# A gated recurrence and a bilinear layer: products moved off GpSimd, inverse scans restarted, weight loads on another queue

## The chip, the cores and the metric

The kernel runs on one core of one Trainium2 chip. The metric is the time of one execution on the device, in microseconds (us). Engines go by the profile's names: PE (TensorE, matrix products), DVE (VectorE), ACT (ScalarE), POOL (GpSimd), SP (SyncE, which here only issues transfers). A "q" behind an engine's name is its queue of issued transfers.

## The reference

Two layers in a row. For 4 batches and 8 heads, 768 steps of a recurrence with a state of 48 x 48, then a layer without a nonlinearity on 3072 tokens of 384 values, with 1536 inner channels:

```python
f = 1.0 / (1.0 + np.exp(-f_logit))            # f_logit about 2.0 +- 0.5
for t in range(768):
    state = f[:, :, t, :, None] * state + np.einsum('bhd,bhe->bhde', k[:, :, t], v[:, :, t])
    y[:, :, t] = np.einsum('bhd,bhde->bhe', q[:, :, t], state)
x = y.transpose(0, 2, 1, 3).reshape(4 * 768, 8 * 48)
out = ((x @ w_a) * (x @ w_b)) @ w_out
```

The three weight matrices arrive as 64-bit floats, everything else as 32-bit floats. All arithmetic is 32-bit.

## The kernel before

**Recurrence.** The work is cut into 16 units (`unit`): one batch, one half of the sequence (384 steps) and four heads, with two heads side by side on the partitions (48 of each 64) and two in the free dimension. A unit's tiles f, k, q and v lie in one of four sets. The decay is written as a quotient: q is multiplied by the running product of f, k by the running product of 1/f, both scaled to stay in range, so that the sums over steps become matrix products over chunks of 64. `front(u)` prepares a unit in three stages:

- stage 1 (L213 to L217): two sigmoids on ACT, of x and of -x - 75; from the second, POOL makes 1 + 1/odds, an approximation of 1/f (`inv`, L216), and its product with f (`fix`, L217), both 768 columns wide;
- stage 2 (L219 to L224): ACT turns `fix` into 2 - f * inv, a correction; DVE scans f (two scans of 384 steps, L222); POOL multiplies q by the scanned f (L224);
- stage 3 (L228, L229): DVE scans `inv` with the factor `fix` (two scans of 384) and multiplies k by it.

`scores` (L257, masked by DVE in L273), `turn` (transposes of k, L284, copied by ACT), `gains` (L303, states summed by DVE in L317 to L326), `within` (L336) and `across` (L356) are the matrix products of a unit. `across` copies y out of PSUM on ACT (L367) into a tile with one buffer and sends it with transfers on SP's queue (L381) into `xT`, the input of the second layer.

**Second layer.** `ffn(blk)` works on eight blocks of 384 tokens. In twelve steps it forms a and b for 128 inner channels (L396: six products for `w_b`, six for `w_a`, PSUM from a ring of four tiles), copies b on ACT (`b_sb`, L404) and multiplies on DVE (`ab`, L406, a product of one operand in PSUM and one in SBUF). Then come the products with `w_out` (L416), 72 in a block, whose results ACT copies out (L426).

**Weights.** `from_double` makes 32-bit floats out of 36 pieces of 128 x 384 64-bit floats (12 of `w_b`, 12 of `w_a`, alternating, then 12 of `w_out`). From the upper words ACT takes absolute value and sign (L166, L167), POOL clamps (L168); two iterations later DVE shifts, masks, scales the lower words and adds (L173 to L176); ACT takes the absolute value once more (L177); one iteration later POOL multiplies by the sign into the weights (L180). `load_weights` issues a piece's load on SP's queue (L154) into one of five buffers, which is free again when L175 has read it.

**Order.** It is written out by hand, and each engine and queue works in the order of the program. The first part prepares units 0 to 2, with a few calls of `convert`, which runs the conversion until n pieces are done. In block 0 `convert` stays some pieces ahead of the step (`min(2 * i + 6, ...)`), while `slot(u)` spreads the front of unit u + 1 and the products of unit u over the steps: six calls a unit, one unit in 7.5 steps. Blocks 1 to 7 go on with the slots alone. At the end a flag that `check_held` has computed decides whether a slower, safe version of the recurrence (`by_levels`) runs; here it does not.

## Time and profile before

| | us |
|---|---|
| median of 3 runs (lowest to highest) | 728.22 (727.71 to 728.41) |
| the profiled execution, as timed | 727.83 |
| its span in the trace | 726.1 |

| engine | busy us | share of the span | instructions |
|---|---|---|---|
| PE | 641.3 | 88% | 4770 |
| DVE | 274.3 | 38% | 467 |
| ACT | 183.5 | 25% | 343 |
| POOL | 149.3 | 21% | 140 |

The page has one execution. Its busy shares are means over stages with different limits, so the slices and stretches of the span matter more here than the sums. "L173" is line 173 of the kernel; a bracket behind an instruction tells how long its engine was idle before it and what ended that. An instruction's length contains the time that it waits for a port once it has started.

### The profile page before, as it was taken

To read this page: it belongs to the slowest core of one execution; us is meant where nothing else is said; L and a number is where in the kernel's file an instruction comes from. 1 tells how busy PE (TensorE), PEld (TensorE's weight loads), DVE (VectorE), ACT (ScalarE), POOL (GpSimd) and SP (SyncE) were. 2 spreads that over 40 slices of the span, in tenths; PEclk is the share of its full clock that TensorE was granted. 3 is DMA by queue.
4 is the path that set the end of the run, shared out by engine and by line. 5 is a ranking of instruction groups with operands and counts; after the bars stand their busy time and mean duration, and the time that the engine had idled before them with its cause. 6 is when DMAs were issued, how large, how long until landed. Compare 5 with 4: busy or idle time off the path is not lost.

```text
span 726.1 us, 11432 instructions
## 1 busy us (share of the span) xinstructions
PE 641.3 (88%) x4770; PEld 390.9 (54%) x4770; DVE 274.3 (38%) x467; ACT 183.5 (25%) x343; POOL 149.3 (21%) x140
## 2 busy tenths in 40 slices
PE   0424875879999999999999999999999999999996
PEld 0423433445566665665665666666666666555553
DVE  8947888889333302322242214131333011001100
ACT  4333446444221202221212122211212011111100
POOL 8635464456201002100102010100110000000000
PEclk9955998799999999999999999999999999999999
DMA  8835324630403030304030401121000000010000
GB/s 212 223 99 130 112 88 124 179 96 32 116 12 71 27 89 0 83 9 106 1 83 0 104 13 41 42 70 46 8 12 20 31 0 18 8 42 0 1 12 25
DMA packets 34300, 43.29 MB, mean 60 GB/s; under 512 B 4032, under 2 KB 32704, under 8 KB 34240
## 3 DMA queue, kind: packets, MB, share of 16 engines
q1 hardware_dynamic: 34240, 42.48, 22.0%
q8 instruction: 39, 0.64, 0.4%
q14 instruction: 21, 0.17, 0.1%
HBM read 33.03 MB, written 4.72 MB: 52 GB/s over the span
## 4 chain that ended last, share of the span: by engine, by line
PE 74%; DVE 16%; ACT 3%; POOL 2%; DMA 2%; issue 2%; SPq 0%; ACTq 0%; POOLq 0%
PE f L396 45%; PE f L416 23%; DVE h L176 3%; DVE r L175 3%; DVE r L174 2%; DVE h L173 2%; DMA k_in<-in_k_dram 2%; PE ps_y L336 2%; DVE inv L228 1%; PE ps_x L257 1%; PE ps_y L356 1%; DVE f_in L222 1%; PE ps_x L303 1%; PE ps_x L284 1%; DVE st L319 1%
## 5 line engine op out<-in xcount | busy, mean ns | idle before, releaser
L396 PE MATMUL f<-xT,w_b 128*128 128x384 f32 x576 | 212.4, 507 | 14.9 <-ACT b_sb L404 14.9
L396 PE MATMUL f<-xT,w_a 128*128 128x384 f32 x576 | 201.7, 486 | 0.0
L416 PE MATMUL f<-w_out,ab 128*128 128x384 f32 x576 | 190.5, 488 | 4.7 <-POOL w_out L180 3.1
L406 DVE TENSOR_TENSOR ab<-f,b_sb 128x384 f32<-128x384 f32 x96 | 53.6, 558 | 329.9 <-PE f L396 311.6
L396 PEld LDWEIGHTS f<-xT,w_b 128*128 128x128 f32 x576 | 109.7, 196 | 88.3 <-POOL w_a L180 11.2
L416 PEld LDWEIGHTS f<-w_out,ab 128*128 128x128 f32 x576 | 108.4, 190 | 81.6 <-POOL w_out L180 6.2
L396 PEld LDWEIGHTS f<-xT,w_a 128*128 128x128 f32 x576 | 109.9, 191 | 77.3 <-issue 1.6
L404 ACT COPY b_sb<-f 128x384 f32<-128x384 f32 x96 | 45.7, 476 | 228.1 <-PE f L396 228.1
L216 POOL TENSOR_SCALAR inv<-inv 128x768 f32<-128x768 f32 x16 | 14.6, 914 | 236.5 <-ACT inv L214 236.4
L426 ACT COPY o_sb<-f 128x384 f32<-128x384 f32 x24 | 11.5, 478 | 167.8 <-PE f L416 162.2
L224 POOL TENSOR_TENSOR q_in<-q_in,f_in 128x768 f32<-128x768 f32 x16 | 30.6, 1915 | 107.6 <-DVE f_in L222 102.1
L257 PE MATMUL ps_x<-q_in,k_in 48*64 48x64 f32 x720 | 15.5, 238 | 41.4 <-POOL q_in L224 19.8
L257 PEld LDWEIGHTS ps_x<-q_in,k_in 48*64 48x64 f32 x720 | 13.9, 152 | 41.9 <-POOL q_in L224 19.8
L177 ACT ACTIVATE h<-h 128x384 f32<-128x384 f32 x36 | 18.8, 523 | 69.8 <-DVE h L176 69.7
L228 DVE TENSOR_TENSOR_SCAN inv<-inv,fix 128x384 f32<-128x384 f32 x32 | 33.9, 1100 | 5.4 <-ACT fix L219 5.4
L168 POOL TENSOR_SCALAR h<-h 128x384 f32<-128x384 f32 x36 | 22.9, 638 | 53.6 <-ACT h L166 51.3
L222 DVE TENSOR_TENSOR_SCAN f_in<-f,zero 128x384 f32<-128x384 f32 x32 | 32.4, 1054 | 2.1 <-ACT inv L214 2.1
L217 POOL TENSOR_TENSOR fix<-f,inv 128x768 f32<-128x768 f32 x16 | 31.2, 1950 | 1.3
L319 DVE TENSOR_TENSOR st<-st,ps_x 128x96 f32<-128x96 f32 x80 | 20.3, 253 | 24.3 <-PE ps_x L303 21.8
L367 ACT COPY y<-ps_y 64x384 f32<-64x384 f32 (+1 forms) x48 | 22.8, 474 | 21.0 <-PE ps_y L356 16.1
L176 DVE TENSOR_TENSOR h<-h,r 128x384 f32<-128x384 f32 x36 | 26.8, 746 | 1.2
L175 DVE SCALAR_TENSOR_TENSOR r<-raw,r 128x384 f32<-128x384 uint32 x36 | 25.3, 703 | 1.2
(56 smaller groups left out, 351.1 us busy)
## 6 DMA issues: line engine op xcount, KB each, us to landing
f_in<-in_f_logit_dram SPq DMA_DIRECT2D x32, 144.0 KB, 2.9
k_in<-in_k_dram SPq DMA_DIRECT2D x32, 144.0 KB, 3.4
q_in<-in_q_dram SPq DMA_DIRECT2D x32, 144.0 KB, 3.9
v_in<-in_v_dram SPq DMA_DIRECT2D x16, 288.0 KB, 4.5
raw<-in_moe_w_b_dram SPq DMA_DIRECT2D x12, 384.0 KB, 3.6
raw<-in_moe_w_a_dram SPq DMA_DIRECT2D x12, 384.0 KB, 3.5
raw<-in_moe_w_out_dram SPq DMA_DIRECT2D x12, 384.0 KB, 3.0
out_dram<-o_sb SPq DMA_DIRECT2D x24, 192.0 KB, 1.9
```

Of the source, the lines that this page charges most:

```text
L175: nc.vector.scalar_tensor_tensor(out=r, in0=lo, scalar=2.0**-52, in1=r, op0=ALU.mult, op1=ALU.mult)
L176: nc.vector.tensor_tensor(h, h, r, ALU.add)
L217: nc.gpsimd.tensor_tensor(fix, f, inv, ALU.mult)
L222: nc.vector.tensor_tensor_scan(x[:, c], f[:, c], zero.broadcast_to((128, BLK)), math.exp(MIDDLE), ALU.mult, ALU.add)
L224: nc.gpsimd.tensor_tensor(halves(t["q"]), halves(t["q"]), x, ALU.mult)
L228: nc.vector.tensor_tensor_scan(inv[:, c], inv[:, c], fix[:, c], math.exp(-MIDDLE), ALU.mult, ALU.mult)
L257: nc.tensor.matmul(ps[h][SUB * p:SUB * p + SUB, o:o + SUB], lhsT=kf[r, tokens(n, c, p)], rhs=qf[r, tokens(n, c, p)], start=True, stop=True,)
L319: nc.vector.tensor_tensor(st[:, j], before, new, ALU.add)
L396: nc.tensor.matmul(ps[nm], lhsT=w[:, kt, ft * 128:ft * 128 + 128], rhs=x[:, kt], start=kt == 0, stop=kt == NKT - 1,)
L404: nc.scalar.copy(b_sb, ps["b"])
L406: nc.vector.tensor_tensor(ab[ft], ps["a"], b_sb, ALU.mult)
L416: nc.tensor.matmul(o[tg], lhsT=ab[ft][:, tg * 128:tg * 128 + 128], rhs=w_out[:, ft], start=ft == 0, stop=ft == NFT - 1,)
```

## The change

- `from_double`: ACT's second absolute value and POOL's product by the sign are gone. ACT makes the upper half of a word with the sign bit alone (`bit`, a third ACT pass with 16-bit output), POOL subtracts the bias of the exponent from the upper 16 bits of the clamped words (a second pass with one input), DVE's first operation shifts and puts the bit in, so it has two tensor inputs, and DVE's last one writes the weights. The conversion is one iteration shorter, `load_weights` comes one iteration later, and `convert` is called with smaller numbers.
- `load_weights`: from the fifth piece on, loads are issued on ACT's queue.
- `front`: `fix` is gone, with the POOL product, the ACT pass and the tile. The inverses are scanned in chunks of 128 steps, each restarted from the reciprocal of the scanned f at the end of the chunk before (DVE). The product for q moves from POOL in stage 2 to DVE in stage 3. The second sigmoid also sums its outputs (for `check_held`). 24 takes the place of 75 in its argument.
- `y` has two buffers; in units 0 and 1 half of its transfers are issued on ACT's queue.
- In the start-up the fronts of units 0 and 1 no longer alternate: unit 0 goes through all stages and on to its scores first, and the conversions begin behind the scores and transposes of unit 1.

```diff
     def load_weights():
...
-            nc.sync.dma_start(out=raw, in_=src)
+            (nc.scalar if len(raws) > 3 else nc.sync).dma_start(out=raw, in_=src)
...
     def from_double(dst, raw, shape):
...
-        h, sign = (sb4.tile([128, PIECE], FP32, tag=n, name=n) for n in ("h", "sign"))
+        i = nth[0] % len(signs)
+        nth[0] += 1
+        sign, bit = signs[i]
+        h = sb4.tile([128, PIECE], FP32, tag="h", name="h")
+        upper = h.bitcast(U16).rearrange("p (n two) -> p n two", two=2)[:, :, 1]
         nc.scalar.activation(h, hi.bitcast(FP32), AF.Abs)
         nc.scalar.activation(sign, hi.bitcast(FP32), AF.Sign)
+        nc.scalar.activation(
+            bit.bitcast(U16).rearrange("p (n two) -> p n two", two=2)[:, :, 1], sign, AF.Relu, scale=-32768.0
+        )
         nc.gpsimd.tensor_scalar(h, h, HI_MAX, HI_MIN, ALU.min, ALU.max)
+        nc.gpsimd.tensor_scalar(upper, upper, 1.0, -float(HI_BIAS), ALU.mult, ALU.add)
         yield
         yield
...
-        nc.vector.tensor_scalar(hu, hu, 3, 0x40000000, ALU.logical_shift_left, ALU.bitwise_xor)
+        nc.vector.scalar_tensor_tensor(
+            out=hu, in0=hu, scalar=3, in1=bit, op0=ALU.logical_shift_left, op1=ALU.bitwise_or
+        )
         nc.vector.tensor_scalar(ru, hu, 0xFF800000, None, ALU.bitwise_and)
         nc.vector.scalar_tensor_tensor(out=r, in0=lo, scalar=2.0**-52, in1=r, op0=ALU.mult, op1=ALU.mult)
-        nc.vector.tensor_tensor(h, h, r, ALU.add)
-        nc.scalar.activation(h, h, AF.Abs)
-        yield
-        h, sign = (x.rearrange("p (k n) -> p k n", k=shape[0]) for x in (h, sign))
-        nc.gpsimd.tensor_tensor(dst, h, sign, ALU.mult)
+        h, r = (x.rearrange("p (k n) -> p k n", k=shape[0]) for x in (h, r))
+        nc.vector.tensor_tensor(dst, h, r, ALU.add)
     def conversion():
...
-            load_weights()
-            yield n - 2
+            if n:
+                load_weights()
+            yield n - 1
     def front(u):
...
-        nc.scalar.activation(inv, x, AF.Sigmoid, bias=less, scale=-1.0)
-
-        nc.gpsimd.tensor_scalar(inv, inv, math.exp(K_EXP), 1.0, ALU.mult, ALU.add)
-        nc.gpsimd.tensor_tensor(fix, f, inv, ALU.mult)
-        yield
-        nc.scalar.activation(fix, fix, AF.Identity, bias=two, scale=-1.0)
+        nc.scalar.activation(inv, x, AF.Sigmoid, bias=less, scale=-1.0, accum_out=tails[:, u:u + 1])
+        nc.gpsimd.tensor_scalar(inv, inv, EXP_K, 1.0, ALU.mult, ALU.add)
+        yield
...
-        nc.gpsimd.tensor_tensor(halves(t["q"]), halves(t["q"]), x, ALU.mult)
-        yield
+        yield
+        start = sb2.tile([128, 2, NC - 1], FP32, tag="start", name="start")
+        nc.vector.reciprocal(start, t["f"].rearrange("p n (c m) -> p n c m", m=C)[:, :, 0:NC - 1, C - 1])
         for n in range(2):
-            c = slice(n * BLK, n * BLK + BLK)
-            nc.vector.tensor_tensor_scan(inv[:, c], inv[:, c], fix[:, c], math.exp(-MIDDLE), ALU.mult, ALU.mult)
+            for c in range(NC):
+                w = slice(n * BLK + c * C, n * BLK + c * C + C)
+                first = start[:, n, c - 1:c] if c else math.exp(-MIDDLE)
+                nc.vector.tensor_tensor_scan(inv[:, w], inv[:, w], none[:, 0:C], first, ALU.mult, ALU.add)
+        nc.vector.tensor_tensor(halves(t["q"]), halves(t["q"]), x, ALU.mult)
         nc.vector.tensor_tensor(halves(t["k"]), halves(t["k"]), inv, ALU.mult)
     def across(u):
...
-        y = sb1.tile([128, 2 * NC, 2, SUB], FP32, tag="y", name="y")
+        y = sb2.tile([128, 2 * NC, 2, SUB], FP32, tag="y", name="y")
...
-                    nc.sync.dma_start(out=xT[blk][p:p + w, kt], in_=y[row:row + w, n])
+                    queue = nc.scalar if u < NQ and (n + h) % 2 else nc.sync
+                    queue.dma_start(out=xT[blk][p:p + w, kt], in_=y[row:row + w, n])
     with tc.manual_schedule():
...
         next(fronts[0])
-        next(fronts[1])
         next(fronts[0])
         next(fronts[1])
-        convert(1)
         scores(0)
         turn(0, True)
-        convert(2)
+        convert(0)
+        next(fronts[1])
         within(0)
         gains(0)
         scores(1, True)
         turn(1, True)
-        convert(3)
+        convert(1)
         across(0)
         within(1)
         gains(1)
         next(fronts[2])
-        convert(4)
+        convert(2)
         across(1)
         next(fronts[2])
         next(fronts[2])
         slots = {s: slot(s) for s in range(NQ, NU + 1)}
         next(slots[NQ])
-        convert(6)
+        convert(4)
...
-                    convert(min(2 * i + 6, 2 * NFT) if i < NFT - 2 else NFT + i + 4)
+                    convert(min(2 * i + 4, 2 * NFT) if i < NFT - 1 else NFT + i + 3)
```

## Rows read from the trace of the kernel before

**Rows 1.** Page, span in 40 equal slices: busy tenths of TensorE and VectorE.

```profile
PE   0424875879999999999999999999999999999996
...
DVE  8947888889333302322242214131333011001100
```

**Rows 2.** Stretches: length, busy us (instructions) of PE, PEld, DVE, ACT, POOL, clock, DMA.

```profile
81.28:158.73 77.45, 54.25 (x321) 31.07 (x320) 64.66 (x105) 39.81 (x82) 42.91 (x45) 0.87 0.42 124
158.73:186.95 28.22, 25.06 (x165) 14.00 (x166) 26.77 (x43) 11.44 (x23) 14.79 (x14) 1.00 0.21 59
186.95:726.10 539.15, 533.04 (x3692) 323.29 (x3691) 120.24 (x227) 100.46 (x183) 44.41 (x30) 1.00 0.14 35
```

**Rows 3.** Groups of VectorE, 24 to 187 us: count | busy us, mean ns | idle before.

```profile
L176 DVE TENSOR_TENSOR h<-h,r 128x384 f32<-128x384 f32 x36 | 26.8, 746 | 1.2
L175 DVE SCALAR_TENSOR_TENSOR r<-raw,r 128x384 f32<-128x384 uint32 x36 | 25.3, 703 | 1.2
L173 DVE TENSOR_SCALAR h<-h 128x384 uint32<-128x384 uint32 x36 | 20.4, 566 | 0.0
L174 DVE TENSOR_SCALAR r<-h 128x384 uint32<-128x384 uint32 x36 | 19.3, 536 | 1.2
L228 DVE TENSOR_TENSOR_SCAN inv<-inv,fix 128x384 f32<-128x384 f32 x8 | 9.1, 1182 | 5.4 <-ACT fix L219 5.4
...
L406 DVE TENSOR_TENSOR ab<-f,b_sb 128x384 f32<-128x384 f32 x12 | 6.7, 558 | 11.5 <-ACT b_sb L404 11.5
```

**Rows 4.** Order of time, 78 to 82 us: start us, length us, instruction [idle before].

```profile
78.20 0.35 DVE L173 TENSOR_SCALAR h<-h 128x384 uint32<-128x384 uint32 x1
...
78.99 0.56 DVE L175 SCALAR_TENSOR_TENSOR r<-raw,r 128x384 f32<-128x384 uint32 x1
...
79.37 0.54 POOL L168 TENSOR_SCALAR h<-h 128x384 f32<-128x384 f32 x1 [3.75 <-ACT h L166]
...
79.58 0.74 DVE L176 TENSOR_TENSOR h<-h,r 128x384 f32<-128x384 f32 x1
79.61 0.37 SPq L154 DMA_DIRECT2D raw<-in_moe_w_a_dram  x1
...
80.36 0.52 ACT L177 ACTIVATE h<-h 128x384 f32<-128x384 f32 x1 [0.62 <-DVE h L176]
...
81.28 0.56 DVE L406 TENSOR_TENSOR ab<-f,b_sb 128x384 f32<-128x384 f32 x1 [0.96 <-ACT b_sb L404]
```

**Rows 5.** Order of time, 89 to 94 us: VectorE operations beside GpSimd's.

```profile
89.75 0.89 POOL L216 TENSOR_SCALAR inv<-inv 128x768 f32<-128x768 f32 x1 [1.72 <-ACT inv L214]
89.97 1.06 DVE L176 TENSOR_TENSOR h<-h,r 128x384 f32<-128x384 f32 x1
...
93.25 1.10 POOL L180 TENSOR_TENSOR w_b<-h,sign 128x384 f32<-128x384 f32 x1
93.54 1.23 DVE L175 SCALAR_TENSOR_TENSOR r<-raw,r 128x384 f32<-128x384 uint32 x1
```

**Rows 6.** Order of time, 295 to 301 us: a front's third stage and the scores.

```profile
296.02 1.80 DVE L228 TENSOR_TENSOR_SCAN inv<-inv,fix 128x384 f32<-128x384 f32 x2
...
297.85 0.96 DVE L229 TENSOR_TENSOR k_in<-k_in,inv 128x768 f32<-128x768 f32 x1
...
299.95 0.88 PE L257 MATMUL ps_x<-q_in,k_in 48*64 48x64 f32 x48
```

**Rows 7.** Groups of VectorE, 81.28 to 158.73 us: the scans of f.

```profile
L222 DVE TENSOR_TENSOR_SCAN f_in<-f,zero 128x384 f32<-128x384 f32 x2 | 1.8, 941 | 0.0
```

**Rows 8.** Order of time, 47 to 55 and 184 us: waits for y, fix and `w_out`.

```profile
47.28 3.12 SPq L381 DMA_DIRECT2D xT<-y  x5
...
52.23 1.46 ACT L367 COPY y<-ps_y 128x384 f32<-128x384 f32 x3 [4.33 <-DMA xT<-y]
...
54.68 0.96 DVE L228 TENSOR_TENSOR_SCAN inv<-inv,fix 128x384 f32<-128x384 f32 x1 [5.43 <-ACT fix L219]
...
184.75 2.20 PE L416 MATMUL f<-w_out,ab 128*128 128x384 f32 x6 [1.72 <-POOL w_out L180]
```

More of the change, by code (lines that the diff above doesn't have):

```diff
@@ L21 @@
 HI_MIN, HI_MAX = (struct.unpack("f", struct.pack("I", x))[0] for x in (0x38000000, 0x47EFFFFF))
+HI_BIAS = 0x3800
 R = 64
 SUB = 64
-K_EXP = 75.0
+K_EXP = 24.0
+EXP_K = math.exp(K_EXP) * (1 + 1.8e-7)
+TAIL_MAX = math.exp(-17)
 MIDDLE = 34.0
@@ L88, in by_quotients @@
     fixedp = ctx.enter_context(tc.tile_pool(name="fixed", bufs=1))
-    sb1 = ctx.enter_context(tc.tile_pool(name="sb1", bufs=1))
     sb2 = ctx.enter_context(tc.tile_pool(name="sb2", bufs=2))
@@ L111, in by_quotients @@
     less = fixed([128, 1], "less")
-    two = fixed([128, 1], "two")
+    signs = [
+        (fixed([128, PIECE], f"sign{i}"), fixedp.tile([128, PIECE], U32, tag=f"bit{i}", name=f"bit{i}"))
+        for i in range(3)
+    ]
+    tails = fixed([128, NU], "tails")
     held = fixed([128, NU, 2], "held")
@@ L144, in pieces @@
             yield w_out[:, ft:ft + 1], moe_w_out[ft * 128:ft * 128 + 128].unsqueeze(1), (1, DM)
-    todo, raws = list(pieces()), []
+    todo, raws, nth = list(pieces()), [], [0]
     def load_weights():
@@ L211, in front @@
         x = halves(t["f"])
[L212 removed]
+        f, inv = (sb2.tile([128, 2 * BLK], FP32, tag=n, name=n) for n in ("f", "inv"))
         nc.scalar.activation(f, x, AF.Sigmoid)
[L214 to L217 removed]
+        nc.scalar.activation(inv, x, AF.Sigmoid, bias=less, scale=-1.0, accum_out=tails[:, u:u + 1])
+        nc.gpsimd.tensor_scalar(inv, inv, EXP_K, 1.0, ALU.mult, ALU.add)
         yield
[L219 removed]
+        none = zero.broadcast_to((128, BLK))
         for n in range(2):
             c = slice(n * BLK, n * BLK + BLK)
[L222 removed]
+            nc.vector.tensor_tensor_scan(x[:, c], f[:, c], none, math.exp(MIDDLE), ALU.mult, ALU.add)
         nc.vector.tensor_tensor(held[:, u], t["f"][:, :, BLK - 1], least, ALU.is_ge)
[L224 removed]
         yield
+        start = sb2.tile([128, 2, NC - 1], FP32, tag="start", name="start")
+        nc.vector.reciprocal(start, t["f"].rearrange("p n (c m) -> p n c m", m=C)[:, :, 0:NC - 1, C - 1])
         for n in range(2):
[L227 to L228 removed]
+            for c in range(NC):
[3 more added lines that the diff above has]
+        nc.vector.tensor_tensor(halves(t["q"]), halves(t["q"]), x, ALU.mult)
         nc.vector.tensor_tensor(halves(t["k"]), halves(t["k"]), inv, ALU.mult)
@@ L453, in check_held @@
     def check_held():
-        n = NU * 2
-        some = fixedp.tile([128, 1], FP32, tag="some", name="some")
-        nc.vector.reduce_sum(some, held.rearrange("p u j -> p (u j)"), axis=mybir.AxisListType.X)
+        n = NU * 3
+        fits = fixed([128, NU], "fits")
+        some = fixed([128, 2], "some")
+        nc.vector.tensor_scalar(fits, tails, TAIL_MAX, None, ALU.is_le)
+        nc.vector.reduce_sum(some[:, 0:1], fits, axis=mybir.AxisListType.X)
+        nc.vector.reduce_sum(some[:, 1:2], held.rearrange("p u j -> p (u j)"), axis=mybir.AxisListType.X)
+        nc.vector.tensor_tensor(some[:, 0:1], some[:, 0:1], some[:, 1:2], ALU.add)
         ps = ps_x
-        nc.tensor.matmul(ps[0:1, 0, 0:1], lhsT=some, rhs=ones, start=True, stop=True)
+        nc.tensor.matmul(ps[0:1, 0, 0:1], lhsT=some[:, 0:1], rhs=ones, start=True, stop=True)
         nc.vector.tensor_scalar(bad, ps[0:1, 0, 0:1], 128.0 * n, None, ALU.is_lt)
@@ L463, in by_quotients @@
         nc.scalar.preload_act_table_set("sigmoid_and_others")
-        for x, value in ((less, -K_EXP), (two, 2.0), (zero, 0.0), (least, math.exp(MIDDLE - DECAY_MAX)), (ones, 1.0)):
+        for x, value in ((less, -K_EXP), (zero, 0.0), (least, math.exp(MIDDLE - DECAY_MAX)), (ones, 1.0)):
             nc.gpsimd.memset(x, value)
@@ L486, in by_quotients @@
         next(fronts[1])
+        for _, bit in signs:
+            nc.gpsimd.memset(bit, 0)
         make_identity(nc, ident)
```

5 lines of the change are left out of this document (2 added, 3 removed).

## The prediction

> **What bounds the kernel now.** I read the slices of the page first, then the busy time of each engine in stretches, then the groups of VectorE in the slow stretch, then the order of time inside one step of it. The slices split the span in two [rows 1]. From about 187 us on TensorE (PE) is at 9 tenths or more in every slice: it is the bound, and the other engines have room. Ahead of that it is at 2 to 8 tenths while VectorE (DVE) stands at 8 or 9 nearly everywhere. The stretches say the same in numbers [rows 2]. Between 81.28 and 158.73 us, the twelve steps of the first feed-forward block, PE is busy 54.25 of 77.45 us and DVE 64.66. Between 158.73 and 186.95 us (the products with `w_out` of that block) both are close to full, 25.06 and 26.77 of 28.22 us. After 186.95 us PE is busy 533.04 of 539.15 us at a granted clock of 1.00, the 2.4 GHz level. The matmuls of that last part are not changed, so time is won where DVE converts weights, and whatever is won there moves the last part forward as a whole.
>
> In the slow stretch four DVE operations on 36 pieces of weights take most of the time: 26.8, 25.3, 20.4 and 19.3 us [rows 3]. Together that is 91.8 us, and with about 3.6 us of short gaps between them (1.2 before three of the four lines) 95.4 us, 2.65 us a piece. DVE also sat idle for 11.5 us before the product `ab`, always behind ScalarE's (ACT's) copy `b_sb` [rows 3].
>
> The order of time shows what a piece costs when nothing disturbs it [rows 4]: from the start of L173 (78.20) to the start of L176 (79.58) is 1.38 us, and a clean L176 would take 0.56, with its last 0.1 under the next start: 1.84 us. The rest, 0.81 us, is waiting inside the instructions while GpSimd (POOL) works. A product on POOL of 1.10 us stretches L175 from 0.56 to 1.23, and a pass with one input of 0.89 us stretches L176 to 1.06 [rows 5]; the shorter pass L168 stretches it to 0.74 [rows 4].
>
> **The change part by part.** Sums are made against the profiled execution: span 726.1 us, 727.83 us as timed, so 1.73 us lie around the span. The median of the runs shown is 728.22.
>
> Part 1, conversion. Gone are ACT's second absolute value (L177) and POOL's product by the sign (L180). New are an ACT pass that writes the sign bit, a POOL pass over 16-bit halves, and a second input in DVE's first operation. That operation goes from 0.35 us [rows 4] to what another 384-wide operation with two inputs and unsigned words takes, 0.56 (L175, same group): +0.21, so a clean piece is 2.05 us. Then the waits for POOL. The 0.67 us of a product goes (L175 at 1.23). The 0.18 of L168 stays (0.74 against 0.56). The new 16-bit pass is nowhere in the trace. Its nearest row is L168, a pass of the same count with one input: 0.18. Its upper bound is the product, 0.67; its lower is nothing, if it always falls beside the `ab` product, which reads PSUM. I take the near end, a little up: 0.39 for both passes, 2.44 us a piece (2.1 to 2.9). 36 x (2.65 - 2.44) = 7.6 us won.
>
> The rule that speaks against this part is in the Trainium skill, "SBUF — State Buffer", section "Who interferes with whom": a VectorE instruction with two SBUF inputs contends with any GpSimd instruction that reads SBUF, and the later of the two waits. By it the passes with one input go on blocking, and DVE's first operation becomes one that can be blocked on its second input. Were it not so, the piece would be 2.05 us; the 1.06 us beside L216 [rows 5] agrees with the rule.
>
> Part 2, the step's end. Now DVE waits 0.96 us before each `ab`: L177 waits for L176 and only then does ACT copy `b_sb` [rows 4]. Afterwards ACT's queue holds, in that place, the issue of a weight load that waits for L175, one operation earlier. A load's issue took 0.37 us on SP's queue [rows 4]; on ACT it is not in the trace (0 to 0.9 us). L175's end + 0.37 + the copy, about 0.46 (it and L177 lie between 80.36 and 81.28), against L175's end + 0.59 for L176: some 0.4 us with the semaphores. 12 x (0.96 - 0.40) = 6.7 us won.
>
> Part 3, the fronts. On DVE the new q product is as large as the k product, 0.96 us [rows 6]. The scans of the inverses go from two of 384 to six of 128, the same 768 elements. Two took 1.80 [rows 6] with 0.94 for one [rows 7], so 0.86 apart; of that 0.80 scales with length if a short operation's fixed part is about 0.06. Six are 1.6 + 6 x 0.06 + 0.1 = 2.05 us. If instead the 0.14 that a 128-wide scan may keep is paid in full, it is six times 0.41, 2.5. The reciprocals of four values: about 0.2. So +0.96 + 0.25 + 0.2, 1.4 us a front. Against it: the two-input POOL products vanish (`fix`, q) that stretch the scans in the start-up from 0.94 to a mean of 1.18 [rows 3] and hold others up besides. For the five fronts that lie ahead of the last piece I take the two as equal: 0, with +/-4 us.
>
> Part 4, early stalls. At 54.68 DVE had sat 5.43 us behind `fix`, which stood on ACT behind the copies of y, which waited 4.33 us for the transfers out of the single y buffer; these began at 47.28 behind a weight load on SP's queue [rows 8]. Double buffering, the end of `fix` and the load on ACT's queue take this whole stall away: 5.4 us. Late next is the first conversion, which now stands behind both score tiles: three ACT passes and two POOL passes of about 0.5 [rows 4] run before DVE has its first words, some 2 us. 3.4 us won.
>
> The move of the loads is the second place where a rule can be held against the trace. The Trainium skill, "DMA: Bandwidth & Descriptors", section "Issuing engines are not separate DMA queues", says that issuing from more engines saves only the sequencer's time. So I count nothing for faster transfers, only the in-order wait at 47.28.
>
> Part 5, what the move costs ACT. Behind a load's issue that waits for DVE stand ACT's passes for later pieces, the `b_sb` copies, the sigmoids of a front, the copies of kT and y. ACT is busy 39.81 of 77.45 us in the stretch [rows 2]; 24 issues of 0.37 add 9. That mostly fits, but where a front's two sigmoids stand ahead of `b_sb` DVE waits for ACT: an estimate of 2.5 us lost.
>
> Part 6, the last piece. PE waits 1.72 us for POOL's last product [rows 8]; it will wait for DVE directly: 1.6 us won.
>
> Part 7, the part bound by PE. A front's third stage sits between two `ab` there. Its first scan starts at 296.02, k is ready at 298.81, and the scores start at 299.95 [rows 6]: room of 1.1 us. The new stage is 0.2 + 2.05 + 0.96 + 0.96 = 4.2 us with gaps (4.1 to 4.9), so k is ready at 300.2 and PE waits 0.3 to 1.0 us. This holds for every second unit, five times after 187 us: 2.0 us lost (1.4 to 5).
>
> Sum: -7.6 - 6.7 + 0 - 3.4 + 2.5 - 1.6 + 2.0 = -14.8. Span 711.3, timed 713.0 us. A floor: in 158.73 to 186.95 PE has 25.06 us of work of its own, so at most 3.2 us can be won there, whatever DVE saves.
>
> **The rivals.**
> A. POOL's one-input passes fall beside `ab` and waits and cost DVE nothing: 2.05 us a piece. That is another 36 x 0.39 = 14, of which those pieces that run beside a full PE give little back: about 12 to 13, 700 us. For it: L406 reads PSUM. Against it: 1.06 us in [rows 5].
> B. The 16-bit pass is as dear as a product and blocks for 0.67: 0.48 more on 36 pieces, 17 us, 730 us: the POOL wait has only changed its name. For it: no row shows a strided 16-bit pass. Against it: it has one input and half the bytes.
> C. Slower: a scan pays its cost once per instruction and not per element, so that a 128-wide one takes as long as a 384-wide one. Six are then 5.2 us in place of 2.05. That adds 3.1 us to five fronts in the start-up and, as PE already waits for k, 3.1 to each of five units afterwards: 31 us, 744 us. It decides from 0.25 us more a scan on (15 us over 60 scans), a scan of some 0.58 us. Against it: two lengths of plain operations here, 384 in 0.56 and 768 in 0.96, scale with their elements.
> D. It doesn't do what it says: the load's issue on ACT, waiting for DVE, holds `b_sb` up as long as L177 did. Then the 6.7 us of part 2 stay: 720 us.
>
> **How the numbers follow.** Forecast with its spread 0.58, D 0.10, A 0.14, B 0.10, C 0.07, 0.01 for something else that is slow. A measurement can tell 0.2% (1.5 us) from no change. Faster: forecast, A and D, 0.82. Within 0.2%: most of B, 0.07. Slower: C and the upper half of B, 0.11. The range 699 to 727 holds A, the forecast, D and the clean bounds of parts 3 and 7, and leaves out B and C.
>
> **What would show it.** L173 with two inputs at 0.56 or more, the four conversion lines near 88 us in sum (A: 74, B: 105); the wait of `ab` for `b_sb` near 5 us; the wait for `fix` gone; 128-wide scans at 0.33 to 0.41; PE idle before L257 some 0.3 to 1.0 us, five times; the first block done near 170 in place of 187 us. I am wrong if ACT, with waits ahead of `b_sb`, takes DVE's place as the bound.

## The result, and the profile after

| | before | after |
|---|---|---|
| median (lowest to highest), us | 728.12 (727.71 to 728.41) | 705.84 (704.70 to 706.96) |
| the profiled execution, as timed | 727.83 | 705.12 |
| its span | 726.1 | 703.4 |

The ratio of the times is 0.969 (0.9675 to 0.9713). The forecast was 713.0, a gain of 14.8 us; the span became 22.7 us shorter. Sign and range held, and the sum was 7.9 us too small.

The slices of the page after, in the form of [rows 1]:

```profile
PE   1519868789999999999999999999999999999996
...
DVE  8679999994343124231434024231514111001100
```

VectorE (DVE) stands at 9 from the fourth to the ninth slice and falls to 4 in the tenth, which begins at 158 us; in [rows 1] it falls in the eleventh, at 182. From there on TensorE (PE) is at 9 tenths or more but for the last slice, as before. The stretches, cut at the same places of the program as [rows 2] (start of block 0, start of its products with `w_out`, start of block 1) with the start-up in the first row; the columns are those of [rows 2]:

```profile
0.00:64.35 64.35, 27.74 (x593) 21.32 (x594) 51.91 (x105) 26.45 (x50) 25.73 (x42) 0.79 0.75 182
64.35:133.80 69.45, 52.41 (x323) 30.00 (x321) 65.63 (x115) 44.73 (x86) 32.05 (x44) 0.90 0.49 141
133.80:163.06 29.26, 26.34 (x164) 14.76 (x165) 28.09 (x57) 13.45 (x26) 10.13 (x14) 0.94 0.46 118
163.06:703.40 540.34, 534.18 (x3693) 323.85 (x3691) 133.30 (x291) 93.30 (x184) 8.34 (x10) 1.00 0.13 34
```

The start-up ended at 81.28 us and now ends at 64.35: 16.9 us won. The twelve steps of block 0 took 77.45 and take 69.45: 8.0 won. The products with `w_out` took 28.22 and take 29.26, the rest 539.15 and 540.34: 1.0 and 1.2 lost. Sum: 22.7. (The cut at 186.95 in [rows 2] lies 0.16 us behind the first product of block 1, which starts at 186.79; cut there, as after, these two losses are 1.2 and 1.0.) So all of the gain lies where DVE is the bound. Part of the start-up's share is only work put off: 6 pieces have gone through DVE by then in place of 9.

The groups of DVE from 23.3 to 160 us, to be held against [rows 3] (columns as there):

```profile
L193 DVE SCALAR_TENSOR_TENSOR r<-raw,r 128x384 f32<-128x384 uint32 x36 | 24.8, 690 | 1.2
L189 DVE SCALAR_TENSOR_TENSOR h<-h,bit 128x384 uint32<-128x384 uint32 x36 | 21.0, 584 | 1.3 <-POOL h L184 1.3
L192 DVE TENSOR_SCALAR r<-h 128x384 uint32<-128x384 uint32 x36 | 15.3, 426 | 1.2
L195 DVE TENSOR_TENSOR w_a<-h,r 128x384 f32<-128x384 f32 x12 | 9.1, 757 | 0.4
L237 DVE TENSOR_TENSOR_SCAN f_in<-f,zero 128x384 f32<-128x384 f32 x8 | 8.3, 1079 | 1.7 <-ACT inv L230 1.7
L195 DVE TENSOR_TENSOR w_b<-h,r 128x384 f32<-128x384 f32 x12 | 8.1, 677 | 0.4
L195 DVE TENSOR_TENSOR w_out<-h,r 128x384 f32<-128x384 f32 x12 | 7.6, 637 | 0.4
L428 DVE TENSOR_TENSOR ab<-f,b_sb 128x384 f32<-128x384 f32 x12 | 6.7, 557 | 1.6 <-PE f L418 0.4
...
L337 DVE COPY st<-ps_x 128x96 f32<-128x96 f32 x2 | 0.5, 253 | 4.1 <-PE ps_x L323 4.1
```

The four conversion lines are 85.9 us in sum (before 91.8); L195 appears as three groups because it writes the weights themselves. `ab` (L428) was idle for 11.5 us and is for 1.6. L193 and L195 are not at their undisturbed length (0.56 [rows 4, 5]): they still take 0.69 and 0.64 to 0.76 in the mean.

Here is the account of DVE up to the end of its last conversion operation. The conversion counts its operations without their overlap of about 0.1 us; "early stalls" are the idle times over 0.3 us that are not ahead of `ab`; the fronts contain the small comparisons for `check_held`. A line of this table tells where DVE's time fell, not which edit brought it.

| | before us | after us | won |
|---|---|---|---|
| conversion, 36 pieces | 88.9 | 83.2 | 5.7 |
| waits of `ab` for `b_sb` and PE | 11.5 | 1.6 | 9.9 |
| fronts (scans, products, reciprocals, comparisons) | 36.5 | 33.6 | 2.9 |
| early stalls | 14.9 | 10.0 | 5.0 |
| last conversion operation ends at | 183.0 | 159.5 | 23.5 |

After that the way to block 1 takes 3.55 us (before 3.76), and the rest 1.0 more: 23.5 + 0.2 - 1.0 = 22.7.

The order of time inside one step, as [rows 4] has it for before:

```profile
128.65 0.71 POOL L183 TENSOR_SCALAR h<-h 128x384 f32<-128x384 f32 x1 [1.46 <-ACT h L177]
129.03 0.74 DVE L193 SCALAR_TENSOR_TENSOR r<-raw,r 128x384 f32<-128x384 uint32 x1
...
129.44 0.81 POOL L184 TENSOR_SCALAR h<-h 128x384 uint16<-128x384 uint16 x1
129.80 0.33 ACTq L161 DMA_DIRECT2D raw<-in_moe_w_out_dram  x1
129.80 0.80 DVE L195 TENSOR_TENSOR w_out<-h,r 128x384 f32<-128x384 f32 x1
130.18 0.48 ACT L426 COPY b_sb<-f 128x384 f32<-128x384 f32 x1 [0.49 <-DVE r L193]
...
130.69 0.56 DVE L428 TENSOR_TENSOR ab<-f,b_sb 128x384 f32<-128x384 f32 x1
```

Both passes of GpSimd (POOL) stretch the DVE operation that runs beside them: L193 to 0.74, by the clamp L183, and L195 to 0.80, by the 16-bit pass L184, from 0.56 each. ScalarE (ACT) issues the load when L193 is done and copies `b_sb` next (130.18 to 130.66). It is finished just as the stretched L195 ends (130.60), and `ab` starts at 130.69.

### The profile page after: what moved, and what is told of

The parts are those of the page before. It is cut to its first block, busy times and chain, and to the rows that moved or that the text cites. A ratio compares the mean times of both kernels' runs of the same rounds, so it can differ in the third digit from the quotient of the medians.

```text
span 703.4 us, 11473 instructions
## 1 busy us (share of the span) xinstructions
PE 640.7 (91%) x4770; PEld 389.9 (55%) x4770; DVE 278.9 (40%) x566; ACT 177.9 (25%) x343; POOL 76.2 (11%) x110
## 3 DMA queue, kind: packets, MB, share of 16 engines
q1 hardware_dynamic: 24224, 29.60, 16.9%
## 4 chain that ended last, share of the span: by engine, by line
PE 78%; DVE 13%; DMA 4%; ACT 2%; issue 1%; ACTq 1%; POOL 0%; SPq 0%; DVEq 0%; POOLq 0%
PE f L418 48%; PE f L438 24%; DVE r L193 3%; DVE h L189 2%; DVE r L192 2%; DVE f_in L237 1%; PE ps_y L356 1%; PE ps_y L376 1%; PE ps_x L277 1%; PE ps_x L304 1%; DMA raw<-in_moe_w_b_dram 1%; PE ps_x L323 1%; DVE w_b L195 1%; DVE inv L247 1%; DMA v_in<-in_v_dram 1%
## 5 line engine op out<-in xcount | busy, mean ns | idle before, releaser
L418 PE MATMUL f<-xT,w_b 128*128 128x384 f32 x576 | 209.7, 501 | 6.9 <-ACT b_sb L426 6.9
L428 DVE TENSOR_TENSOR ab<-f,b_sb 128x384 f32<-128x384 f32 x96 | 53.5, 557 | 308.8 <-PE f L418 307.6
L448 ACT COPY o_sb<-f 128x384 f32<-128x384 f32 x24 | 11.5, 479 | 175.3 <-PE f L438 173.9
L183 POOL TENSOR_SCALAR h<-h 128x384 f32<-128x384 f32 x36 | 25.9, 720 | 66.5 <-ACT h L177 66.0
L237 DVE TENSOR_TENSOR_SCAN f_in<-f,zero 128x384 f32<-128x384 f32 x32 | 29.9, 974 | 1.7 <-ACT inv L230 1.7
L177 ACT ACTIVATE h<-raw 128x384 f32<-128x384 f32 x36 | 20.0, 557 | 38.5 <-DVE r L193 24.8
L184 POOL TENSOR_SCALAR h<-h 128x384 uint16<-128x384 uint16 x36 | 27.0, 751 | 3.0
L247 DVE TENSOR_TENSOR_SCAN inv<-inv,start,zero 128x128 f32<-128x128 f32 x64 | 26.9, 461 | 0.0
L193 DVE SCALAR_TENSOR_TENSOR r<-raw,r 128x384 f32<-128x384 uint32 x36 | 24.8, 690 | 1.2
L180 ACT ACTIVATE bit<-sign 128x384 uint16<-128x384 f32 x36 | 22.9, 636 | 1.3
L189 DVE SCALAR_TENSOR_TENSOR h<-h,bit 128x384 uint32<-128x384 uint32 x36 | 21.0, 584 | 1.3 <-POOL h L184 1.3
```

Of the source, the lines that this page charges most:

```text
L180: nc.scalar.activation(bit.bitcast(U16).rearrange("p (n two) -> p n two", two=2)[:, :, 1], sign, AF.Relu, scale=-32768.0)
L183: nc.gpsimd.tensor_scalar(h, h, HI_MAX, HI_MIN, ALU.min, ALU.max)
L184: nc.gpsimd.tensor_scalar(upper, upper, 1.0, -float(HI_BIAS), ALU.mult, ALU.add)
L189: nc.vector.scalar_tensor_tensor(out=hu, in0=hu, scalar=3, in1=bit, op0=ALU.logical_shift_left, op1=ALU.bitwise_or)
L193: nc.vector.scalar_tensor_tensor(out=r, in0=lo, scalar=2.0**-52, in1=r, op0=ALU.mult, op1=ALU.mult)
L237: nc.vector.tensor_tensor_scan(x[:, c], f[:, c], none, math.exp(MIDDLE), ALU.mult, ALU.add)
```

## The experiments

Each kernel is the changed one with the edit shown, except b_conv. For each the median is given, with the 95% interval of its ratio to the kernel before.

**How POOL's passes cost DVE time (parts 1 and 2, rivals A and B).** Three kernels put one more POOL instruction behind the 16-bit pass of every piece; it writes a spare tile that nobody reads.

```diff
+    spare_tile = fixedp.tile([128, PIECE], mybir.dt.bfloat16, ...)
         nc.gpsimd.tensor_scalar(upper, upper, 1.0, -float(HI_BIAS), ALU.mult, ALU.add)
+        nc.gpsimd.memset(spare_tile, 0.0)                                                # x_memset
+        nc.gpsimd.tensor_scalar(spare_tile, h, HI_MAX, HI_MIN, ALU.min, ALU.max)         # x_onein
+        nc.gpsimd.tensor_tensor(spare_tile, h, sign, ALU.mult)                           # x_twoin
```

> The changed kernel with one more GpSimd instruction per piece of weights, a memset of 128 x 384 into a spare tile, which reads nothing. Port theory (a GpSimd instruction that reads SBUF holds up a VectorE operation with two SBUF inputs or in its fast mode until it is done): a memset costs VectorE nothing, 705.8 us within 1. Rival (what counts is how long GpSimd is busy per piece, or the length of the chain ScalarE - GpSimd - VectorE): about 36 x 0.2 to 0.4 us more, 713 to 720.

> The changed kernel with one more GpSimd pass per piece that reads one 128 x 384 tile (the clamp again, into a spare tile). Port theory: VectorE waits about 0.2 us more per piece, as L195 does beside L184 (0.80 in place of 0.56): 36 x 0.2 = 7 us, a little less where TensorE is the bound, 711 to 714. Rival A of the prediction (one-input passes cost VectorE nothing): 706. Rival of x_memset: the same as the memset.

> The changed kernel with one more GpSimd product of two 128 x 384 tiles per piece, into a spare tile, as long as the sign product that the change took away. Port theory: 0.67 us of VectorE per piece as in the trace of before, 36 x 0.67 = 24 us, less what falls beside the ab product: 722 to 730. If the gain came from elsewhere (queues, buffers, chain): under 712.

Measured: x_memset 705.49 us (0.9683 to 0.9715), nothing against 705.84; x_onein 711.34 (0.9759 to 0.9791), 5.5 slower; x_twoin 726.65 (0.9966 to 0.9986), 20.8 slower. By the spans (703.9, 709.9 and 725.7, against 703.4) a pass with one input costs 6.5 / 36 = 0.18 us a piece and a product 22.3 / 36 = 0.62. Order of time in x_memset, then in x_twoin:

```profile
100.30 0.42 POOL L186 MEMSET spare_tile<- 128x384 bf16 x1
...
100.62 0.56 DVE L197 TENSOR_TENSOR w_b<-h,r 128x384 f32<-128x384 f32 x1
```

```profile
101.02 1.12 POOL L186 TENSOR_TENSOR spare_tile<-h,sign 128x384 bf16<-128x384 f32 x1
...
101.32 1.24 DVE L197 TENSOR_TENSOR w_b<-h,r 128x384 f32<-128x384 f32 x1
```

A DVE operation with two inputs that starts beside a memset takes its clean 0.56. Beside a product it takes 1.24: the product is through at 101.02 + 1.12 = 102.14, the DVE operation at 102.56. So the cost is not "POOL is busy" but "POOL reads", and it is higher with two inputs than with one. The Trainium skill says so in "SBUF — State Buffer", section "Who interferes with whom": a VectorE instruction with two SBUF inputs contends with GpSimd instructions that read SBUF. All three runs agree that reading decides. (The product is also the longer instruction, 1.07 us in the mean against 0.61 for the added pass; the next kernel bears on that.) Nearly the whole gain of the conversion is there to be lost again by one product a piece: the rival that counted one-input passes as free (A) is wrong, and so is the one that counted the 16-bit pass as dear as a product (B).

**One POOL pass fewer.** One 16-bit pass does both the clamp from below and the subtraction; the clamp against weights too large for 32-bit floats is left out.

```diff
-        nc.gpsimd.tensor_scalar(h, h, HI_MAX, HI_MIN, ALU.min, ALU.max)
-        nc.gpsimd.tensor_scalar(upper, upper, 1.0, -float(HI_BIAS), ALU.mult, ALU.add)
+        nc.gpsimd.tensor_scalar(upper, upper, float(HI_BIAS), -float(HI_BIAS), ALU.max, ALU.add)
```

> The changed kernel with one GpSimd pass per piece in place of two: the 16-bit pass takes the lower clamp with it (max, then minus the bias), the first pass is gone; what is left out is the clamp of weights that are too large for 32-bit floats. Port theory: VectorE waits about 0.2 us less per piece, 36 x 0.2 = 7 us, of which the part beside the w_out products gives back little: 699 to 702. If VectorE's waits beside L184 are only moved: 705.

Measured: 699.39 us (0.9595 to 0.9627), 6.4 faster. Not all of that is DVE's: the last conversion operation ends 4.0 us earlier (155.50 against 159.50), and another 1.5 come from PE's clock (below). Its groups of DVE, 16 to 190 us:

```profile
L427 DVE TENSOR_TENSOR ab<-f,b_sb 128x384 f32<-128x384 f32 x19 | 10.6, 558 | 23.3 <-PE f L417 19.4 <-ACT b_sb L425 3.7
...
L194 DVE TENSOR_TENSOR w_out<-h,r 128x384 f32<-128x384 f32 x12 | 6.7, 558 | 0.4
```

L194 (the former L195) of `w_out` is clean at 0.558 us (of `w_b` and `w_a` it takes 0.66 and 0.59). But now DVE waits 3.7 us for `b_sb` (L425). The stretched L195 had hidden the load's issue and the copy; with the stretch gone they show. So part of what part 2 seemed to win was paid for in part 1's line.

The one pass that is left is no short one. It takes 1.79 us in the mean, longer than the two that it replaces (0.72 and 0.75), and yet the four conversion lines fall from 85.9 to 79.3 us in sum, 0.18 a piece. Order of time:

```profile
96.90 1.82 POOL L183 TENSOR_SCALAR h<-h 128x384 uint16<-128x384 uint16 x1 [2.27 <-ACT h L177]
...
97.86 0.56 DVE L192 SCALAR_TENSOR_TENSOR r<-raw,r 128x384 f32<-128x384 uint32 x1
```

L192 reads two tiles and runs at its clean length in the middle of POOL's pass. Where it starts 0.2 to 0.35 us behind the start of such a pass it takes 0.74 (at 99.91, beside a pass from 99.61 on). So neither the length of POOL's instruction nor its end sets the price here; only the first part of this pass holds DVE up. (POOL's spans in the profile are rough.)

**The loads and half of y on SP's queue again, and the y buffer.**

```diff
-            (nc.scalar if len(raws) > 3 else nc.sync).dma_start(out=raw, in_=src)
+            nc.sync.dma_start(out=raw, in_=src)                    # u_loads_sp, u_sp_y_single
...
-        y = sb2.tile([128, 2 * NC, 2, SUB], FP32, tag="y", name="y")
+        y = y1.tile([128, 2 * NC, 2, SUB], FP32, tag="y", name="y")   # bufs=1: u_y_single, u_sp_y_single
...
-                    queue = nc.scalar if u < NQ and (n + h) % 2 else nc.sync
+                    queue = nc.sync                                # u_loads_sp, u_sp_y_single
```

> The changed kernel with all weight loads, and all transfers of y, issued on SP's queue again. Queue theory (the move to ACT's queue took the early stall away, as the prediction had it): transfers of y wait behind loads again, 709 to 711. Order theory (a load is now issued one iteration later, so none waits for a VectorE operation that stands behind the transfers of y in the program): no stall comes back, 705.8 within 1.5; ACT, free of 0.35 us an issue, may even gain a little.

> The changed kernel with one buffer for y. Buffer theory (the second buffer took away the 4.33 us that ACT waited in the kernel before): 708 to 710. Order theory (the transfers of unit 0 now start at 29.2 us, as soon as y is copied, and have landed before the copies of unit 1 at 36.9): 705.8 within 1.

> Both undone: loads and transfers of y on SP's queue, one buffer for y. If the two stand in for each other, so that either alone hides the stall: 709 to 712 here and 706 in the two others. Order theory: 705.8 within 2, since nothing that the transfers wait for has come back.

Measured: u_loads_sp 699.67 us (0.9597 to 0.9629), 6.1 faster than the changed kernel; u_y_single 704.46 (0.9656 to 0.9688), 1.4 faster, but not told apart, as the ranges overlap (703.18 to 704.95 against 704.70 to 706.96); u_sp_y_single 699.83 (0.9599 to 0.9631), the same as u_loads_sp. Neither the second y buffer nor ACT's queue is what took the early stall away: with both undone DVE's wait of 5.43 us [rows 8] does not come back. And the move costs time; neither of the two theories had a gain of 6.1 us in it. Groups of DVE in u_loads_sp, 23.3 to 160 us, then one row of the waits of SP's queue there (whole time, count, longest), then one row of the waits of ACT in the changed kernel up to 165 us:

```profile
L237 DVE TENSOR_TENSOR_SCAN f_in<-f,zero 128x384 f32<-128x384 f32 x8 | 8.6, 1121 | 0.0
...
L428 DVE TENSOR_TENSOR ab<-f,b_sb 128x384 f32<-128x384 f32 x12 | 6.6, 546 | 0.0
```

```profile
SPq L161 <- DVE r L193: 80.4, 28, 9.9
```

```profile
ACT b_sb L426 <- DVE r L193: 7.0, 12, 1.0
```

On SP the loads wait 80.4 us for L193, and only other transfers stand behind them. On ACT the same wait holds `b_sb` up for 7.0 us (12 times) and, in a front, the two sigmoids, behind which POOL and L237 start: the changed kernel's 1.7 us ahead of L237 and 1.6 ahead of L428 are both 0.0 here. These 3.3 us are most of the 4.6 by which the last conversion operation ends earlier (159.51 against 154.94). Another 1.1 lies in `ab` itself: without a wait each of the twelve starts under the end of the operation before it (5.6 us without overlap in place of 6.7). Further, 1.5 us come from PE's clock (below). The Trainium skill, "DMA: Bandwidth & Descriptors", section "Issuing engines are not separate DMA queues", grants a second issuing engine only the sequencer's time; the runs agree, and here that engine had work of its own behind the issue.

**The new conversion alone in the kernel before (part 1 and 2 without the fronts, the queue and the start-up order).** b_conv is the kernel before with `from_double`, `conversion` and `load_weights` of the changed one, loads on SP, and three bit tiles.

```diff
+        nc.scalar.activation(bit.bitcast(U16)...[:, :, 1], sign, AF.Relu, scale=-32768.0)
+        nc.gpsimd.tensor_scalar(upper, upper, 1.0, -float(HI_BIAS), ALU.mult, ALU.add)
...
-        nc.vector.tensor_tensor(h, h, r, ALU.add)
-        nc.scalar.activation(h, h, AF.Abs)
-        yield
-        nc.gpsimd.tensor_tensor(dst, h, sign, ALU.mult)
+        nc.vector.tensor_tensor(dst, h, r, ALU.add)
```

> The kernel before with the new conversion alone (sign bit, no product by the sign, one iteration less, loads one iteration later but still on SP's queue); fronts, y, the written order and the numbers of convert as before. From VectorE's account: some 4 us of waiting for the sign products, 10 to 11 us of waiting of the ab product, 1.5 us behind the last piece, together 16: 712 (709 to 715). If the fronts' products on GpSimd were the main cause: above 718.

Measured: 707.87 us (0.9699 to 0.9736). It alone brings 2.8% of the 3.1% that the whole change brings. Its groups of DVE, 24 to 187 us:

```profile
L193 DVE SCALAR_TENSOR_TENSOR r<-raw,r 128x384 f32<-128x384 uint32 x36 | 25.9, 719 | 1.2
L189 DVE SCALAR_TENSOR_TENSOR h<-h,bit 128x384 uint32<-128x384 uint32 x36 | 21.4, 596 | 1.1 <-POOL h L184 1.1
...
L195 DVE TENSOR_TENSOR w_a<-h,r 128x384 f32<-128x384 f32 x12 | 12.5, 1040 | 0.4
```

I had looked for a part of the gain in those lines, and it isn't there: the four are 95.5 us in sum (the fourth, L192, is 20.4, L195 of the other two matrices 15.3), more than the 91.8 of before. The gain is in the waits: ahead of `ab` DVE waits for ACT no more (11.5 us before), and the 7.6 us it had waited ahead of the fronts' scans are gone too; these were not in the expectation of 712, which is 4 us too long. What the shorter conversion buys is a shorter round trip through ACT and POOL, more than shorter DVE operations.

Why did the lines not get shorter? The sign products are gone, beside which they had been stretched, but the first operation is 0.55 us undisturbed in place of 0.35 (7.2 us over 36 pieces), and there is a second reading pass on POOL. And the fronts' products still fall on them. Order of time in the kernel before, then in b_conv:

```profile
90.71 1.99 POOL L217 TENSOR_TENSOR fix<-f,inv 128x768 f32<-128x768 f32 x1
90.96 1.96 DVE L173 TENSOR_SCALAR h<-h 128x384 uint32<-128x384 uint32 x1
```

```profile
57.57 1.98 POOL L233 TENSOR_TENSOR fix<-f,inv 128x768 f32<-128x768 f32 x1
...
57.92 2.04 DVE L195 TENSOR_TENSOR w_a<-h,r 128x384 f32<-128x384 f32 x1
```

Four operations are stretched in this way in the kernel before (two L173 beside `fix`, two L174 beside the product for q), by 6.2 us in sum, and five in b_conv (three L195, two L192), by 7.5. The changed kernel has none.

u_loads_sp is the run to hold against b_conv: both load on SP, and they differ by the fronts, the start-up order with its numbers of `convert`, two more sign tiles, and the second y buffer, which was worth nothing above. u_loads_sp is 8.2 us faster. Its last conversion operation ends 9.0 us earlier (154.94 against 163.90), and its conversion takes 82.9 us without overlap against 92.6. So the new fronts together with the start-up order are worth some 9 us; in the changed kernel the move of the loads hides half of it. The order was not undone by itself, but 7.5 us stand in the five operations above.

**Is it the round trip?** An ACT pass that waits for DVE's last operation is put back; its result goes nowhere.

```diff
         nc.vector.tensor_tensor(dst, h, r, ALU.add)
+        nc.scalar.activation(spare_tile..., dst, AF.Abs)
```

> The changed kernel with one more ACT pass per piece that waits for VectorE's last operation of that piece (an absolute value into a spare tile), as L177 did in the kernel before. If the wait of the ab product is worth its whole length: 12 times about 0.85 us come back, 9 to 11 us, 715 to 717. If VectorE has other work that fills such a gap, or the copies of b only trade places: under 709.

Measured: 713.11 us (0.9783 to 0.9815), 7.3 slower. The last conversion operation ends 9.6 us later (169.08), as the first theory has it; the time lies under its 715 mostly because PE's clock gives 1.5 back in this run (below). The group of `ab` in DVE, 23.3 to 175 us:

```profile
L430 DVE TENSOR_TENSOR ab<-f,b_sb 128x384 f32<-128x384 f32 x12 | 6.7, 558 | 11.6 <-ACT b_sb L428 11.6
```

The wait is back, 11.6 us, all of it for `b_sb`, as in [rows 3]. So one such pass is enough for the 11.5 us before `ab`, and in b_conv they are gone without it: they came from one ACT pass that stood ahead of `b_sb` and waited for DVE.

**The product for q on POOL again (part 3).**

```diff
+        nc.gpsimd.tensor_tensor(halves(t["q"]), halves(t["q"]), x, ALU.mult)     # stage 2
...
-        nc.vector.tensor_tensor(halves(t["q"]), halves(t["q"]), x, ALU.mult)     # stage 3
```

> The changed kernel with the q product on GpSimd again, in stage 2 as before. VectorE is rid of 0.93 us a front, but a product of 768 columns holds it up for about 1.5 us (L224 in the trace of before): five fronts ahead of the last piece, 5 x 0.6 = 3 us more, minus 0.8 us in the part bound by TensorE, where k is ready earlier: 708 (706 to 710). If VectorE's own work decided alone: 5 us less, 701.

Measured: 708.35 us (0.9714 to 0.9746), 2.5 slower. Order of time:

```profile
40.31 1.80 POOL L239 TENSOR_TENSOR q_in<-q_in,f_in 128x768 f32<-128x768 f32 x1 [2.74 <-DVE f_in L237]
...
40.43 1.97 DVE L248 TENSOR_TENSOR_SCAN inv<-inv,zero 128x128 f32<-128x128 f32 x1
```

A 128-wide scan beside POOL's product takes 1.97 us, clean 0.40, and ends only after it. What DVE saves, 0.93 us a front, it pays in stretched scans, and the conversion takes 87.1 us in place of 83.2. The last conversion operation ends 5.4 us later (164.89). Of that, 1.5 come back by PE's clock (below) and 1.1 in the part bound by PE, so that the forecast of 708 is met by a sum that did not contain the clock.

**What the last feed-forward products wait for (part 6).** This comes out of a row that repeats over the runs. Groups of PE's products with `w_out` around the last pieces: the changed kernel, u_loads_sp and x_abs.

```profile
155.46 7.76 PE L438 MATMUL f<-w_out,ab 128*128 128x384 f32 x18 [1.88 <-DVE w_out L195]
```

```profile
150.90 6.30 PE L438 MATMUL f<-w_out,ab 128*128 128x384 f32 x18 [1.71 <-DVE w_out L195]
```

```profile
165.04 6.30 PE L440 MATMUL f<-w_out,ab 128*128 128x384 f32 x18 [2.31 <-DVE w_out L196]
```

Eighteen products take 7.76 us in the first and 6.30 in the other two. The granted clock tells why. Stretches of 2 us (columns as in [rows 2], the clock is the third number from the end) in the changed kernel, then in u_loads_sp:

```profile
153.00:155.00 2.00, 0.58 (x2) 0.00 (x0) 1.90 (x6) 0.00 (x0) 0.00 (x0) 1.00 0.44 115
155.00:157.00 2.00, 1.54 (x4) 0.97 (x5) 1.90 (x5) 0.00 (x0) 0.00 (x0) 0.80 1.05 245
157.00:159.00 2.00, 2.00 (x5) 1.09 (x4) 1.90 (x5) 0.00 (x0) 0.00 (x0) 0.50 1.07 199
159.00:161.00 2.00, 2.00 (x6) 1.16 (x6) 2.00 (x7) 0.00 (x0) 0.00 (x0) 0.84 0.49 106
```

```profile
149.00:151.00 2.00, 0.29 (x2) 0.11 (x1) 1.90 (x5) 0.00 (x0) 0.00 (x0) 1.00 0.87 241
151.00:153.00 2.00, 2.00 (x7) 1.01 (x7) 1.90 (x5) 0.00 (x0) 0.00 (x0) 1.00 1.08 207
153.00:155.00 2.00, 2.00 (x8) 1.01 (x7) 1.90 (x6) 0.00 (x0) 0.00 (x0) 1.00 0.67 139
```

In the changed kernel PE had waited 1.88 us, then worked, and the granted clock went down to 0.50 (the 1.2 GHz level) between 157 and 159 us. In u_loads_sp it stayed at 1.00 (2.4 GHz) after 1.71 us. From the end of the last conversion operation to block 1 it is 3.55 or 3.56 us in the changed kernel, u_y_single and x_memset, x_onein and x_twoin, in all of which the clock reads 0.50 in that place; it is 2.09 or 2.10 us in f_onepass, u_loads_sp, u_sp_y_single, x_abs, u_q_pool, f_sp_onepass and f_best, where it reads 1.00. The fall costs 1.46 us. So whoever compares two of these runs by their time alone has the clock in the difference: the seven kernels that keep the clock have 1.5 us of it against the changed kernel. b_conv, whose conversion is the new one in the old order, has it too (3.67 us, clock 0.50). The wait was 1.88 or 1.89 us in all six; but its length alone doesn't decide, as x_abs waited 2.31 us and kept its clock. What does is open.

**The best of it.** f_sp_onepass joins u_loads_sp and f_onepass. f_best also converts the second piece before the gains of unit 1, where DVE had waited for PE (4.1 us ahead of L337 above). Both leave the clamp out as f_onepass does.

```diff
         within(1)
+        convert(2)
         gains(1)
         next(fronts[2])
-        convert(2)
```

> The changed kernel with loads and transfers of y on SP's queue and one GpSimd pass per piece (the clamp against weights too large for 32-bit floats is left out). The two gains, 6.1 and 6.4 us, each measured alone, overlap where TensorE is the bound beside the w_out products: 694 to 696. If both took away the same waits: 699.

> f_sp_onepass with the second piece of weights converted ahead of the states of unit 1 (convert(2) in front of gains(1)), into the 4.0 us in which VectorE is idle at 28 us. A piece takes 2.3 us there: 2 us less than f_sp_onepass. If ScalarE or TensorE needs that order: the same or more.

Measured: 693.76 us (0.9507 to 0.9542) and 691.40 (0.9484 to 0.9526), the second 14.4 us faster than the changed kernel. The first lies just under the expected 694 to 696. The first copy of the states in f_sp_onepass, then in f_best:

```profile
33.38 0.26 DVE L336 COPY st<-ps_x 128x96 f32<-128x96 f32 x1 [3.80 <-PE ps_x L322]
```

```profile
32.17 0.26 DVE L336 COPY st<-ps_x 128x96 f32<-128x96 f32 x1 [1.72 <-PE ps_x L322]
```

DVE's wait for PE goes from 3.80 to 1.72 us, and the last conversion operation ends 3.3 us earlier (146.21 against 149.54); the medians are 2.4 apart.

## Why the prediction was right in sign and short in size

The main reading was right: DVE's conversion was the bound, PE's part was untouched, and time won ahead of block 1 moved the rest forward (539.3 us from there to the end before, 540.3 after). Part by part:

- **Part 1** (7.6 forecast in the conversion's lines, 5.9 by the same group sums, 5.7 without overlap). A piece was forecast at 2.44 us and is 2.49, both with gaps (the sign "near 88 us" contains them too; the lines alone were 84.2 forecast and are 85.9). But that it is near is chance, for the edit that was meant does not bring it: b_conv, with the new conversion alone, has these lines 3.7 us longer (92.6 without overlap against 88.9). The 2.65 us a piece of before contained the stretch beside `fix` and the product for q (6.2 us in sum), and the 2.44 left it out, so a gain of part 3 was booked here. The second input was not what makes the first operation blockable either: L173 with its one input was held to 0.57 in the mean against 0.35, and 1.96 beside `fix`; L189 takes 0.58. The 0.39 for both POOL passes was near: 0.18 for the clamp (0.74 against 0.56), 0.24 for the 16-bit pass (0.80 against 0.56). x_onein gives 0.18 for a third one.
- **Part 2** (6.7 forecast, 9.9 measured). I had set issue and copy behind L175 against 0.59 for L176. L195, the operation it had to race, was itself held to 0.80 by POOL. The two terms were not independent: f_onepass, which removes the hold, shows 3.7 us of the wait again, close to the 0.40 x 12 = 4.8 that I had counted. x_abs shows the cause to be the ACT pass: 11.6 us.
- **Part 3** (0 forecast; 2.9 won in the fronts' own lines, some 9 by the edit). This is the term that was mis-sized most. The size of the new instructions was right: a 128-wide scan is 0.40 us long and follows the last by 0.31, six of them take 2.2 us (forecast 2.05 to 2.5) and the reciprocal 0.17. What I gave away too cheaply is the stretch of the operations beside the two-input POOL products, which is gone, and most of it lay on the conversion and not on the fronts: b_conv, with the old fronts, has their own lines 2.6 us shorter already, and u_loads_sp, with the new ones, saves another 9.7 us, all in the conversion. u_q_pool brings one of the two products back and loses 5.4 us up to the last piece.
- **Part 4** (3.4 forecast, 5.0 measured), near in size with the wrong cause named. I gave the stall to the y buffer and to the load on SP's queue ahead of y's transfers. u_y_single and u_sp_y_single put the one buffer back, u_loads_sp and u_sp_y_single the loads on SP's queue, and the stall doesn't come back. b_conv still has both as before, and `fix` and the old start-up order as well, and its scans wait no more. So the stall went with the edit of the conversion. There y of unit 0 is copied by 36.99 us and its transfers are issued from 36.75 on; in the kernel before it is copied by 39.76 and they are issued from 47.28 on [rows 8], behind a load that waits for an L175 which ends at 46.75. That fits the load that is issued one iteration later; it was not taken apart from the shorter chain of the same edit.
- **Part 5** (2.5 lost forecast). Moving the loads to ACT costs 6.1 us (u_loads_sp): 4.6 up to the last piece and 1.5 by the clock. I had the mechanism, load's issue ahead of sigmoids and `b_sb`, but the number was an estimate without a row. With the 12 x 0.40 that part 2 left as remaining wait I had 7.3 for the move in all; that this is near is chance, since the clock is in the 6.1.
- **Part 6** (1.6 forecast, 0.2 measured). The wait for POOL did go: in kernels that keep the clock the way from the last piece to block 1 is 2.09 us against 3.76, 1.67 won. In the changed kernel the clock's fall took 1.46 of it back. The floor that I gave, at most 3.2 us to be won in that stretch, held: it became 1.2 longer.
- **Part 7** (2.0 lost forecast, 1.0 measured). In the stage of a front beside a full PE, order of time:

```profile
272.50 0.17 DVE L242 RECIPROCAL start<-f_in 128x4 f32<-128x4 f32 x1
272.58 0.40 DVE L247 TENSOR_TENSOR_SCAN inv<-inv,zero 128x128 f32<-128x128 f32 x1
...
275.56 0.95 DVE L249 TENSOR_TENSOR k_in<-k_in,inv 128x768 f32<-128x768 f32 x1
...
276.56 0.93 PE L277 MATMUL ps_x<-q_in,k_in 48*64 48x64 f32 x48
```

From 272.50 to 276.51 (k ready) it is 4.0 us, forecast 4.2, and the scores start at 276.56, right behind. From the scores of one unit to those of the next but one it takes 77.68 us (167.73 to 245.41) against 77.48 before: some 0.2 us for every second unit, five times, less than the 0.3 to 1.0 that I had given. In u_q_pool, where the product for q is not in this stage, it is 77.48 again, so the cost is that product's.

Summed with the signs of gains: -5.7 - 9.9 - 2.9 - 5.0 - 0.2 + 1.0 = -22.7, where part 5's loss already lies inside the first four. By edits it reads otherwise. Up to the last conversion operation the new conversion brings 19.1 us (b_conv; 17.7 forecast in parts 1, 2 and 4), the new fronts with the start-up order 9.0 (0 forecast), and the move of the loads loses 4.6 (2.5 forecast). Together that is 23.5. The forecast was short mainly because I took part 3 as a balance of zero, and because I charged part 2 for a wait that another loss was hiding. That the gap is not larger is owed to the move, which costs more than I had counted.

**The rivals.** A (one-input passes free, 700 us) falls with x_onein. B (16-bit pass as dear as a product, 730 us) falls with L195 at 0.80 and not 1.23, and x_twoin shows what it would have looked like: 726.65. C (scans pay by the instruction, 744 us) falls with the scan of 0.40 us. D (the load's issue on ACT takes the place of the old wait, 720 us) is right in that the issue holds ACT up and costs 6.1 us, and wrong in where: `ab` hardly waits in the changed kernel, since DVE is held elsewhere at the time.

## What to carry to other kernels

Before you count a wait as won, ask which other loss lies beside it: removing one uncovers the other, and two terms of the sum may be one. A line that got shorter doesn't tell which edit shortened it: the conversion's lines fell because of the fronts. Run each edit alone. An instruction that waits for a buffer belongs on a queue where nothing stands behind it; SP waited 80 us here and held no engine up, while the loads on ACT cost 6.1 us, 1.5 of them by the clock. Count GpSimd's passes beside a busy VectorE by the tensors that they read: a pass that read none cost nothing, one tensor of 128 x 384 0.18 us and two 0.62 us a piece here. Their length alone is no measure: with one pass of 1.79 us in place of two of 0.72 and 0.75, DVE was held up less.
